# An FFT filter and a two-layer product on one core: the last output tile in one piece, one copy on another engine, and a few pieces moved

## The chip, the cores and the metric

The kernel runs on one core of one Trainium2 chip. The core has several engines that run side by side and wait for one another through semaphores. TensorE multiplies matrices; the profile calls it PE, and PEld for its weight loads. VectorE is called DVE, ScalarE ACT, GpSimd POOL and SyncE SP. In this kernel SP issues the transfers between the on-chip memory and the DRAM, and POOL issues the loads of x and of the weights and the exchanges between partitions.

The metric is device time in microseconds (us). One execution was also taken with a profiler; its "span" reaches from the first to the last instruction.

## What is computed

Two steps, the second on the output of the first (cut to what matters):

```python
def _attn_ref(x, filt_r, filt_i):            # x: (8, 3008, 256)
    X = np.fft.rfft(x, axis=1)
    Y = X * (filt_r + 1j * filt_i)[None]
    return np.fft.irfft(Y, n=x.shape[1], axis=1)

def _moe_ref(x, w_in, w_out, alpha):         # x: (24064, 256), w_in: (256, 2048)
    h = x @ w_in
    g = np.maximum(h, 0.0) + alpha * np.minimum(h, 0.0)
    return g @ w_out
```

Each of 8 batches is filtered along its sequence of 3008 by a Fourier transform, a product with a filter and the transform back. The result, seen as 24064 tokens of 256 numbers, goes through a product to 2048 numbers, a leaky rectifier with its own slope for each of these, and a product back to 256.

## The kernel before

**The filter, in four stages for each batch.** 3008 is 94 x 32, and the transform is split that way.

- Stage a ("first stage") multiplies pieces of x by a table of the 94-point transform: `piece_a` (two products, L184) for batches 1 to 3; `piece_q` (four products, L210, on sums and differences of the two halves of x, which `less` and `plus` make on VectorE) for batches 4 to 7, where the plan calls the batch `split`. Each piece fills two banks of product memory (a tile `hps`) that ScalarE copies to `asb` (L315). There are eight pieces in a batch; after each second one `save_a` or `save_q` writes a quarter of `asb` to DRAM, and `turn_a` loads it back in another order as `at` (L227).
- Stage b: `piece_b` (eight products, L238, into a tile `psF`). VectorE multiplies the result by two forms of the filter (`ww`, L245, and `uu`, L246), and POOL exchanges `ww` between partitions: it is added on the way (L250, batch 1), or copied to `sw` (L252) and added by VectorE eight steps later (L257, `piece_s`).
- Stage c: `piece_c` (eight products, L269, into an `hps` tile). ScalarE copies it to `v`; `turn_c` writes `v` to DRAM (L280), and `load_zt` loads it as `zt` (L288).
- Stage d ("last stage"): `pair_d` (eight products, L293, into `psF`) and a copy to `yT`, the input of the second step, by ScalarE or VectorE.

Batch 0 has its own, earlier form (`First`) without the way through DRAM; its last transposes (`piece_t`, L411) and `pair_d` fall into the first blocks of the second step and use `psF` too.

**The second step** goes by 48 blocks of tokens, twelve for each pair of batches, of 512 tokens each but for the sixth, of 384. A block has 16 steps; step `16 n` is the first of block `n`. In each, `up` makes one slice of h (two products, L579). Two steps share an `hps` tile, which ScalarE copies to `gtb` (L588); VectorE makes the rectifier from it (L591 twice, then L593 after each fourth step). `down` (L647) multiplies `gtb` by `w_out`, 16 products for each tile of 128 tokens, two tiles in one bank of `op`. ScalarE copies it to `osb` (L652), and `store` writes it out (L561). The work of `down` is cut into 16 units for each block, kept in a queue (`units`), and runs during the block after, a unit at a time, through `pop`.

**What sets the order.** All engines run their instructions in program order, and the program is written out by hand: `plan` lists for each step what is put between the products, in the order of the `put` calls. `plan_fft` fills it for a batch: `a_at`, `b_at`, `c_at` and `d_at` are the steps of its eight stage-a pieces, six `piece_b`, six `piece_c` and eight `pair_d`. `psum[step]` counts the pieces of a step that take an `hps` tile; from step 150 on that many units of `down` run before them and as many after them, ahead of the step's own `up`. There are two `hps` tiles, one `psF`, two `op` and three `osb`, each used in turn, so a product that writes a tile waits until the copy from it two (or one) tiles ago is over, and a copy into `osb` waits until the stores of three copies ago have landed.

For the last block `start_down(last)` orders the first three tiles of 128 tokens, and `down_halves` makes the fourth in two halves of 128 columns, each with its own product, copy (L639) and store:

```python
ends = [2, 3] if last else list(range(2, n, 2)) + [n]
...
pop(n + (step in (290, 482)))
...
blk.down_halves(3)
```

Of the kernel before, what the change touches and what calls it, by code (L numbers as in the profile page):

```python
# [11 lines left out]
FP32 = mybir.dt.float32  # L12
# [3 lines left out]
N2 = 32  # L16
NK = 24
D = 256
# [3 lines left out]
AF = mybir.ActivationFunctionType  # L22
# [33 lines left out]
def kernel(  # L56
# [10 lines left out]
    nc = tc.nc  # L67
# [11 lines left out]
    p_osb = ctx.enter_context(tc.tile_pool(name="p_osb", bufs=3))  # L79
# [23 lines left out]
    wout_s = konst.tile([128, 16, D], FP16, name="wout_s")  # L103
# [12 lines left out]
    def load_x(b, c, held=False):  # L116
        xs = p_x.tile([128, 8 * D], FP16, name="xs")
        if held:
            for r in (slice(0, 32), slice(64, 96)):
                nc.vector.memset(xs[r, 0:2], 0.0)  # L120
        if b:
            for r in (slice(0, 48), slice(48, N1)):
                nc.gpsimd.dma_start(out=xs[r], in_=xrow(b, c)[r])  # L123
        else:
            w = 8 * D // (1 + (c == 3))
            for o in range(0, 8 * D, w):
                nc.gpsimd.dma_start(out=xs[0:N1, o : o + w], in_=xrow(b, c)[:, o : o + w])
        return xs

    def load_halves(b, c):  # L130
        lo, hi = (p_x.tile([128, 8 * D], FP16, name="xs") for _ in range(2))
        nc.gpsimd.dma_start(out=lo[0:48], in_=xrow(b, c)[0:48])
        if b + 1 < NB:
            nc.gpsimd.dma_start(out=hi[0:48], in_=bass.AP(
                tensor=x.tensor, offset=x.offset + (b * NFFT + 47 * N2 + 8 * c) * D, ap=[[N2 * D, 48], [1, 8 * D]]))
        else:
            nc.gpsimd.dma_start(out=hi[0:32], in_=xrow(b, c)[47:79])
            nc.gpsimd.dma_start(out=hi[32:47], in_=xrow(b, c)[79:94])
        return lo, hi
# [12 lines left out]
    def banks(wide):  # L152
        if wide:
            return psH.tile([128, 2, 512], FP32, name="hps")
        return psF.tile([128, 2, 512], FP32, name="psF")

    def bank(kind):
        if kind == "o":
            return psO.tile([128, 2, D], FP32, name="op").rearrange("p k d -> p (k d)")
        return banks(kind == "h")[:, 0]  # L160
# [5 lines left out]
    class Fft:  # L166
# [115 lines left out]
                        in_=self.v[p : p + N2, k : k + 8])  # L282

        def load_zt(self):
            ends = (0, 8, 16, 32) if self.b == 2 else range(0, 33, 8)
            for g in range(len(ends) - 1):
                s = slice(ends[g], ends[g + 1])
                nc.sync.dma_start(out=self.zt[:, s], in_=v_dram[self.b, :, s])  # L288

        def inverse(self, pd, g, dh, mh):  # L290
# [217 lines left out]
    for kp in range(12):  # L508
        if 0 < kp < 10:
            f0.piece_b(kp + 2)  # L510
        if kp == 4:
# [5 lines left out]
            for q in range(2):  # L517
                nc.gpsimd.dma_start(
                    out=wout_s[:, 8 * q : 8 * q + 8],
                    in_=moe_w_out[1024 * q : 1024 * q + 1024].rearrange("(j p) d -> p j d", p=128))  # L520
# [27 lines left out]
    for p in range(NB // 2):  # L548
        t = 0
# [1 line left out]
            blocks.append((p, t, tn))  # L551
            t += tn

    def store(p, t0, osb, lane, lo=0, hi=D):
        t = t0
        while t < t0 + 128:
            b, r = 2 * p + t // NFFT, t % NFFT
            g, o = r // NX, r % NX
            n = min(t0 + 128 - t, NX - o)
            row = b * NFFT + (o // 4) * N2 + 4 * g  # L560
            nc.sync.dma_start(  # L561
                out=bass.AP(tensor=out.tensor, offset=out.offset + row * D + lo,
                            ap=[[N2 * D, n // 4], [D, 4], [1, hi - lo]]),
                in_=osb[t - t0 : t - t0 + n, lane, lo:hi])
            t += n

    gturn = [0]
# [1 line left out]
    class Block:  # L569
# [49 lines left out]
        def start_down(self, last, quarters=False):  # L619
            n = self.tn // 128  # L620
            if quarters:
                self.todo = [(s0, s0 + 2, si, k) for k0 in range(0, 16, 4) for s0 in range(0, n, 2)
                             for si in (s0, s0 + 1) for k in range(k0, k0 + 4)]
                return
            ends = [2, 3] if last else list(range(2, n, 2)) + [n]
            half = 12 if last else 8
            self.todo = []
            for s0, s1 in zip([0] + ends, ends):
                for ks in (range(half), range(half, 16)):
                    self.todo += [(s0, s1, si, k) for si in range(s0, s1) for k in ks]  # L630

        def down_halves(self, si):
            for lo in range(0, D, 128):
                op = bank("h")[:, 0:128]
                for k in range(16):
                    nc.tensor.matmul(op, self.gts[k][:, 128 * si : 128 * si + 128], wout_s[:, k, lo : lo + 128],
                                     start=(k == 0), stop=(k == 15))
                osb = p_osb.tile([128, 2, D], FP32, name="osb")
                nc.scalar.activation(osb[:, 0, lo : lo + 128], op, AF.Copy)  # L639
                store(self.p, self.t0 + 128 * si, osb, 0, lo, lo + 128)  # L640

        def down(self, q):
            n = self.tn // 128
# [16 lines left out]
    plan, psum = {}, {}  # L660

    def put(step, fn, *args):
        plan.setdefault(step, []).append((fn, args))

    def put_h(step, fn, *args):
        put(step, fn, *args)
        psum[step] = psum.get(step, 0) + 1

    def plan_fft(b, a_at, ta, x_at, b_at, add, c_at, d_at):
        f = Fft(b)  # L670
        split = b > 3
        for q in range(6):
            put_h(c_at[q], f.piece_c, q)
            if q % 2 == 1:
                put(c_at[q] + 1, f.turn_c, q // 2)
        put(c_at[5] + (2 if b == 1 else 1), f.load_zt)
        for q in range(6):
            put(b_at[q], f.piece_b, q, not add)
            if add:
                put(b_at[q] + add, f.piece_s, q)  # L680
        for i in range(8):
            put_h(a_at[i], f.piece_q if split else f.piece_a, i)
        for c in range(4):
            put(a_at[2 * c + 1] + split, f.save_q if split else f.save_a, c)
            if b in (2, 3):
                put(x_at[c], lambda b=b, c=c: xc.update({(b, c): load_x(b, c, b == 3 and c > 1)}))
            if split:
                x0, x1, x2 = x_at[c]
                put(x0, lambda b=b, c=c: xc.update({(b, c): load_halves(b, c)}))
                put(x1, f.less, c)  # L690
                put(x2, f.plus, c)
        w = NK // len(ta)
        for q, t in enumerate(ta):
            put(t, f.turn_a, nc.sync, w * q, w * q + w)
        for i in range(8):
            put(d_at[i], f.pair_d, i, on_act)
# [11 lines left out]
    for i in (6, 7):  # L708
        put(3, lambda i=i: on_dve(*f0.half_t(i, "o")))
    put(7, f0.pair_d, 2, on_dve)  # L710
    for g, ts, ds, te, de in ((2, (19, 24), (28, 30), (on_dve, on_dve), (on_dve, on_dve)),
                              (3, (32, 34), (36, 38), (on_act, on_act), (on_act, on_act))):
        for i in range(2):
            put(ts[i], f0.piece_t, 2 * g + i, te[i])
            put(ds[i], f0.pair_d, 2 * g + i, de[i])
# [7 lines left out]
    def d_steps(p):  # L723
# [1 line left out]

    plan_fft(1, range(16, 32, 2), [31] * 4, None, (40, 46, 52, 58, 63, 68), 0, (52, 58, 64, 70, 76, 80),
             (93, 95, 98, 101, 114, 121, 142, 154))
    plan_fft(2, (48, 54, 60, 66, 72, 74, 82, 86), [90] * 4, (39, 45, 51, 57),
             (106, 116, 126, 136, 148, 158), 7, (116, 126, 136, 148, 158, 172), d_steps(96))
    for b in range(3, NB):  # L730
        p = 96 * (b - 1)
        if b == 3:
            a_at = (106, 112, 118, 124, 130, 132, 140, 144)
            x_at = (62, 69, 113, 123)
            ta = (155, 166)
        else:
            a_at = [p - 96 + t for t in (-34, -22, 2, 2, 14, 26, 38, 50)]
# [6 lines left out]
    def pop(n):  # L744
        for _ in range(n):
            if units:
                blk, q = units.popleft()
                blk.down(q)

    last = 0  # L750
    blk = Block(0, 0, 512)
# [10 lines left out]
    step = 16  # L762

    for p, t0, tn in blocks[1:]:
        blk = Block(p, t0, tn)
        for j in range(16):
            n = psum.get(step, 0)
            if step < 150:
                pop({16: 0, 18: 2}.get(step, 1 if n else 0))
            else:  # L770
                pop(n)
            for fn, args in plan.pop(step, ()):
                fn(*args)
            if step >= 150:
                pop(n + (step in (290, 482)))
            blk.up(j)
            if n:
                last = step
            else:
                soon = any(t in psum for t in range(step + 1, step + 14))  # L780
                if not (step >= 150 and step % 2 and step - last > 2 and soon and len(units) < 18 - j):
                    pop(1)
            step += 1
        blk.start_down(step == 16 * len(blocks))
        units.extend((blk, q) for q in range(16))
    pop(len(units))
    blk.down_halves(3)
    assert not plan


# [28 lines left out]
```

## Time and profile before

| | |
|---|---|
| time, median of 3 runs | 768.16 us (766.91 to 768.26) |
| profiled execution | 767.84 us |
| its span | 766.1 us |
| PE busy | 756.4 us (99%) |
| DVE busy | 634.2 us (83%) |
| ACT busy | 582.6 us (76%) |
| POOL busy | 146.5 us (19%) |
| L647 (`down`) | 2992 products, 273 ns each |
| L579 (`up`) | 1504 products, 375 ns each |
| DMA | 100.04 MB, mean 131 GB/s |

How to read it: products overlap, so the duration of one is longer than the distance to the next one's start. "L647" is line 647 of the kernel before; `op<-wout_s,gtb` means that `op` is written from `wout_s` and `gtb`. In a timeline each line has the start, the duration, the engine, the line and the operation; like instructions in a row are drawn together (x4), and brackets hold the idle time before them and what ended it. SPq is SP's queue of transfers; its durations are those of issuing, not of the transfer.

### The profile page before, as it was taken

How to read it: one execution, taken by the hardware profiler on the slowest of the kernel's cores; microseconds unless marked ns; L12 is line 12 of the kernel's file. 1: busy time of each engine (PE TensorE's matmuls, PEld its weight loads, DVE VectorE, ACT ScalarE, POOL GpSimd, SP SyncE). 2: the span in 40 equal slices, each digit the busy share in tenths (PEclk: the TensorE clock that was granted, in tenths of full speed). 3: DMA queues.
4: the chain of work that ended last, by engine and by line, in shares of the span. 5: the costliest groups of instructions: out<-in, count | busy, mean ns of one | idle time of the engine just before them, and what ended most of it. 6: DMA issues, size and time to landing. Idle time of an engine off the chain costs nothing.

```text
span 766.1 us, 16640 instructions
## 1 busy us (share of the span) xinstructions
PE 756.4 (99%) x6569; PEld 507.7 (66%) x6569; DVE 634.2 (83%) x1163; ACT 582.6 (76%) x673; POOL 146.5 (19%) x277
## 2 busy tenths in 40 slices
PE   8999999999999999999999999999999999999997
PEld 4676667666666667666666666766666666766666
DVE  4898975889789998899888998899877888676673
ACT  4788787888788787887878787788767777776663
POOL 6620740231211220122202122112201212000000
PEclk9999999999999999999999999999999999999999
DMA  9996996565762469543864438533562213511011
GB/s 163 163 238 170 165 207 202 149 167 138 181 160 71 122 159 196 135 113 86 191 191 104 118 104 196 161 85 118 138 169 78 84 57 91 152 36 38 32 42 56
DMA packets 97518, 100.04 MB, mean 131 GB/s; under 512 B 12086, under 2 KB 83526, under 8 KB 97152
## 3 DMA queue, kind: packets, MB, share of 16 engines
q1 hardware_dynamic: 82416, 69.50, 31.2%
q0 software_dynamic: 15024, 29.49, 21.4%
q8 instruction: 51, 0.84, 0.4%
q14 instruction: 27, 0.22, 0.1%
HBM read 55.02 MB, written 46.66 MB: 133 GB/s over the span
## 4 chain that ended last, share of the span: by engine, by line
PE 89%; DVE 5%; DMA 3%; POOL 1%; ACT 1%; issue 1%; SPq 0%; DVEq 0%; ACTq 0%; POOLq 0%
PE op L647 40%; PE hps L579 39%; PE psF L293 2%; PE hps L269 2%; PE psF L238 1%; DVE m L591 1%; DVE gtb L593 1%; DMA xs<-in_x_dram 1%; PE hps L184 1%; PE hps L210 1%; DMA sw<-ww 1%; DVE gtb L616 1%; DMA filt_s<-in_filt_r_dram 1%; PE hps L602 1%; DVE m L615 1%
## 5 line engine op out<-in xcount | busy, mean ns | idle before, releaser
L588 ACT ACTIVATE gtb<-hps 128x1024 f16<-128x1024 f32 (+1 forms) x376 | 377.4, 1006 | 131.9 <-PE hps L579 129.5
L647 PE MATMUL op<-wout_s,gtb 128*128 128x256 f16 x2992 | 428.9, 273 | 0.0
L579 PE MATMUL hps<-yT,win_s 128*128 128x512 f16 (+1 forms) x1504 | 417.6, 375 | 0.0
L647 PEld LDWEIGHTS <-gtb 128*128 128x128 f16 x2992 | 289.3, 98 | 163.3 <-issue 10.7
L591 DVE TENSOR_SCALAR m<-gtb,alm_s 128x512 f16<-128x512 f16 (+1 forms) x752 | 227.1, 346 | 96.0 <-ACT gtb L588 94.5
L593 DVE TENSOR_TENSOR gtb<-gtb,m 128x2048 f16<-128x2048 f16 (+1 forms) x188 | 226.1, 1203 | 10.3
L579 PEld LDWEIGHTS <-win_s 128*128 128x128 f16 x1504 | 142.5, 98 | 54.7 <-issue 4.7
L252 POOL DMA_DIRECT2D sw<-ww x144 | 71.9, 508 | 414.3 <-DVE ww L245 399.5
L652 ACT ACTIVATE osb<-op 128x512 f32<-128x512 f32 x96 | 56.3, 586 | 11.0 <-PE op L647 9.9
L315 ACT ACTIVATE asb<-hps 128x1024 f16<-128x1024 f32 (+1 forms) x56 | 56.7, 1020 | 7.1 <-PE hps L184 5.5
L315 ACT ACTIVATE v<-hps 128x1024 f16<-128x1024 f32 (+1 forms) x43 | 43.5, 1011 | 10.9 <-PE hps L269 10.9
L245 DVE TENSOR_TENSOR ww<-psF,filts_s 128x1024 f16<-128x1024 f32 x42 | 51.2, 1218 | 0.6 <-PE hps L579 0.4
L246 DVE TENSOR_TENSOR uu<-psF,filt_s 128x1024 f16<-128x1024 f32 x42 | 51.0, 1215 | 0.0
L315 ACT ACTIVATE yT<-psF 128x752 f16<-128x752 f32 (+1 forms) x59 | 46.5, 788 | 1.6 <-PE psF L293 1.5
L293 PEld LDWEIGHTS <-zt 96*128 96x128 f16 x504 | 28.1, 98 | 6.2 <-issue 0.7
L293 PE MATMUL psF<-wi_s,zt 96*128 96x94 f16 x448 | 27.9, 205 | 0.0
L257 DVE TENSOR_TENSOR uu<-uu,sw 128x1024 f16<-128x1024 f16 x36 | 24.6, 682 | 1.6 <-DMA sw<-ww 1.6
L250 POOL DMA_DIRECT2D uu<-ww x24 | 19.2, 1160 | 28.8 <-DVE uu L246 22.8
L123 POOL DMA_DIRECT2D xs<-in_x_dram x24 | 18.4, 1003 | 12.3 <-issue 4.3
L194 DVE TENSOR_TENSOR xs<-xs 47x2048 f16<-47x2048 f16 x16 | 19.5, 1220 | 0.4
L198 DVE TENSOR_TENSOR xs<-xs 47x2048 f16<-47x2048 f16 x16 | 19.4, 1210 | 0.0
L269 PE MATMUL hps<-uu,twi_s 64*64 64x256 f16 x336 | 17.3, 281 | 0.3 <-DVE uu L257 0.2
(104 smaller groups left out, 269.5 us busy)
## 6 DMA issues: line engine op xcount, KB each, us to landing
out_dram<-osb SPq DMA_DIRECT2D x127, 128.0 KB
v_dram<-v SPq DMA_DIRECT2D x84, 128.0 KB
zt<-v_dram SPq DMA_DIRECT2D x26, 384.0 KB
sw<-ww POOLq DMA_DIRECT2D x144, 64.0 KB, 2.6
xs<-in_x_dram POOLq DMA_DIRECT2D x40, 192.0 KB, 6.7
at<-a_dram SPq DMA_DIRECT2D x40, 192.0 KB
a_dram<-asb SPq DMA_DIRECT2D x32, 192.0 KB
a_dram<-asb SPq DMA_DIRECT2D x12, 384.0 KB
```

Of the source, the lines that this page charges most:

```text
L245: nc.vector.tensor_mul(ww, px, fs)
L246: nc.vector.tensor_mul(uu, px, f)
L252: nc.gpsimd.dma_start(out=sw[o : o + 32], in_=ww[i : i + 32])
L269: nc.tensor.matmul(ps[64 * par : 64 * par + 64, e, 256 * h : 256 * h + 256], twi_s[r, 4 * q + 2 * h + par], u[r, par, h], start=True, stop ...
L293: nc.tensor.matmul(ps[:, m], self.zt[:, 8 * g + 4 * mh + m, dh * 128 : dh * 128 + 128], self.wi, start=True, stop=True)
L315: nc.scalar.activation(o, i, AF.Copy)
L579: nc.tensor.matmul(self.hps[:, j % 2, 0:tn], win_s[:, kt, j * 128 : (j + 1) * 128], yT[:, kt, self.t0 : self.t0 + tn], start=(kt == 0), st ...
L588: nc.scalar.activation(g[:, 2 * i : 2 * i + 2], self.hps[:, :, 0:tn], AF.Copy)
L591: nc.vector.tensor_scalar(m[:, 2 * i + h], g[:, 2 * i + h], 0.0, a, OP.min, OP.mult)
L593: nc.vector.tensor_add(g, g, m)
L647: nc.tensor.matmul(self.op[s0][:, si - s0], self.gts[k][:, 128 * si : 128 * si + 128], wout_s[:, k], start=(si == s0 and k == 0), stop=(si ...
L652: nc.scalar.activation(osb[:, 0:m], self.op[s0][:, 0:m], AF.Copy)
```

## The change

Six edits, each small:

1. The fourth tile of the last block is made like the third: 16 products of 256 columns into `op`, one copy, one store. `down_halves` is gone.
2. Of batch 0's four late `pair_d` copies, that of step 28 goes from VectorE to ScalarE.
3. Batch 2's last two stage-a pieces move from steps 82 and 86 to 78 and 82.
4. In batches 4 to 7, piece 2 of stage a is put at the front of its step's list, in steps 194, 290, 386 and 482. There it stands ahead of the `piece_b` of the batch before, with piece 3 still behind it.
5. The additional unit of `down` at steps 290 and 482 is gone. In TensorE's order its three products come back at the end of steps 299 and 491.
6. Batch 2's `zt` is loaded in four quarters like that of the others, not in two quarters and a half.

On TensorE 32 products of 128 columns become 16 of 256; all others stay, some at other places. VectorE has one copy fewer and ScalarE the same number.

```diff
-            ends = (0, 8, 16, 32) if self.b == 2 else range(0, 33, 8)
-            for g in range(len(ends) - 1):
-                s = slice(ends[g], ends[g + 1])
+            for g in range(4):
+                s = slice(8 * g, 8 * g + 8)
                 nc.sync.dma_start(out=self.zt[:, s], in_=v_dram[self.b, :, s])
...
-            ends = [2, 3] if last else list(range(2, n, 2)) + [n]
+            ends = [2, 3, 4] if last else list(range(2, n, 2)) + [n]
...
-        def down_halves(self, si):
-            for lo in range(0, D, 128):
-                op = bank("h")[:, 0:128]
-                for k in range(16):
-                    nc.tensor.matmul(op, self.gts[k][:, 128 * si : 128 * si + 128], wout_s[:, k, lo : lo + 128],
-                                     start=(k == 0), stop=(k == 15))
-                osb = p_osb.tile([128, 2, D], FP32, name="osb")
-                nc.scalar.activation(osb[:, 0, lo : lo + 128], op, AF.Copy)
-                store(self.p, self.t0 + 128 * si, osb, 0, lo, lo + 128)
...
             put_h(a_at[i], f.piece_q if split else f.piece_a, i)
+            if split and i == 2:
+                plan[a_at[2]].insert(0, plan[a_at[2]].pop())
...
-    for g, ts, ds, te, de in ((2, (19, 24), (28, 30), (on_dve, on_dve), (on_dve, on_dve)),
+    for g, ts, ds, te, de in ((2, (19, 24), (28, 30), (on_dve, on_dve), (on_act, on_dve)),
...
-    plan_fft(2, (48, 54, 60, 66, 72, 74, 82, 86), [90] * 4, (39, 45, 51, 57),
+    plan_fft(2, (48, 54, 60, 66, 72, 74, 78, 82), [90] * 4, (39, 45, 51, 57),
...
-                pop(n + (step in (290, 482)))
+                pop(n)
...
     pop(len(units))
-    blk.down_halves(3)
```

`store` loses the arguments `lo` and `hi` that only the halves used.

More of the change, by code (lines that the diff above doesn't have):

```diff
@@ L552, with store @@
             t += tn
-    def store(p, t0, osb, lane, lo=0, hi=D):
+    def store(p, t0, osb, lane):
         t = t0
@@ L561, in store @@
             nc.sync.dma_start(
-                out=bass.AP(tensor=out.tensor, offset=out.offset + row * D + lo,
-                            ap=[[N2 * D, n // 4], [D, 4], [1, hi - lo]]),
-                in_=osb[t - t0 : t - t0 + n, lane, lo:hi])
+                out=bass.AP(tensor=out.tensor, offset=out.offset + row * D,
+                            ap=[[N2 * D, n // 4], [D, 4], [1, D]]),
+                in_=osb[t - t0 : t - t0 + n, lane])
             t += n
```

## The prediction

> **What bounds the kernel now.** I read the page first (busy times, chain by engine), then the chain's end, then the timeline at each place that the change touches.
>
> ```profile
> PE 756.4 (99%) x6569; PEld 507.7 (66%) x6569; DVE 634.2 (83%) x1163; ACT 582.6 (76%) x673; POOL 146.5 (19%) x277
> ...
> PE 89%; DVE 5%; DMA 3%; POOL 1%; ACT 1%; issue 1%; SPq 0%; DVEq 0%; ACTq 0%; POOLq 0%
> ```
>
> TensorE is busy for 756.4 of 766.1 us and has 89% of the chain. So an edit counts where it opens or closes a gap between products, or behind the last product. Unhindered, an L647 starts every (6.28 - 0.27)/55 = 0.109 us (the 56 from 753.69 on) and an L579 every (1.03 - 0.38)/3 = 0.217; gaps below are counted against that.
>
> The chain's end, then the timeline there (start, duration, engine, what; in brackets the idle time before and what ended it):
>
> ```profile
> 760.29 2.57 DMA out_dram<-osb
> ...
> 762.96 0.28 ACT osb L639
> ```
>
> ```profile
> 759.80 1.95 PE L636 MATMUL hps<-wout_s,gtb 128*128 128x128 f16 x32
> 760.05 0.38 ACT L652 ACTIVATE osb<-op 128x256 f32<-128x256 f32 x1 [1.15 <-PE op L647]
> ...
> 762.96 0.28 ACT L639 ACTIVATE osb<-hps 128x128 f32<-128x128 f32 x1 [1.74 <-DMA out_dram<-osb]
> ```
>
> The last copy waits 1.74 us, not for its products (over at 761.75) but for a store that still reads the output tile which it reuses.
>
> Steps 28 to 30, the one long gap of the first blocks:
>
> ```profile
> 58.70 0.93 DVE L318 CAST yT<-psF 128x752 f16<-128x752 f32 x1
> ...
> 59.69 0.49 PE L293 MATMUL psF<-wif_s,zt 96*128 96x94 f16 x8 [0.49 <-DVE yT L318]
> ...
> 60.65 1.02 ACT L315 ACTIVATE asb<-hps 96x1024 f16<-96x1024 f32 x1 [0.74 <-PE hps L184]
> ```
>
> Around step 93 (batch 1's loads of zt, then its first last-stage product):
>
> ```profile
> 119.84 1.83 SPq L288 DMA_DIRECT2D zt<-v_dram  x4
> ...
> 124.03 0.50 PE L293 MATMUL psF<-wi_s,zt 96*128 96x94 f16 x8
> ```
>
> No wait shows, but the last of the sixteen semaphore updates of the first of these loads is at 123.76: only 0.27 us to spare.
>
> **The change, part by part.**
>
> *Last tile in one piece: -0.88.* Two halves (32 products of 128 columns) become 16 of 256, at the same rate: the last starts at 759.80 + 15 x 0.109 = 761.43 and ends 0.27 later, at 761.71. With one copy fewer, the ring of three output tiles gives the last copy the tile of the copy at 754.81, whose stores have landed by 759.16; the wait goes. The copy starts 0.08 behind the product (760.05 against 759.97) and takes 0.38 like its neighbour: over at 762.17 instead of 763.24, 1.07 sooner. SP is free at 761.86. The store has 128 KB instead of 64: 2.08 us from issue to landing (stores at 749.54 and 761.29) instead of 1.89 (763.27), 0.19 longer. Ends: -1.07 (store as quick as the small one) and -0.39 (as slow as the one at 760.29, 2.57).
>
> *Copy of step 28 by ScalarE: -0.50.* The product's last L293 ends at 57.02 and ScalarE is then free, so the copy starts at 57.06, not at 58.70 behind VectorE's add (L593). It holds ScalarE 0.68 us (spacing of the yT at 318.70 to the next L588), of which 0.43 lay idle there (57.06 to the asb at 57.49): the asb starts at 57.74, the L588 at 58.66 instead of 58.41, over at 59.67. TensorE reaches step 30's L293 at 59.03 and, with psF free, saves 0.66; its L579 at 59.79 finds the bank of that L588 free. Late next is VectorE: the L591 pair now waits for that L588 (59.71), the second copy starts at 60.36 instead of 60.22 and ends at 61.31, and step 32's L411, which needs psF, starts at 61.36 instead of 61.10 (now: 61.76): 0.40 left. The next gap there (0.10 at 64.03, waiting for a zt copy by ScalarE) closes, since ScalarE runs 0.5 ahead: 0.50. Ends: 0 and -0.66. The transfers behind it move along: the save of step 30 goes out 0.15 sooner, and the at loads needed at 70.45 had landed at 69.05.
>
> *Batch 2's pieces at 78 and 82 instead of 82 and 86: +0.26.* Step 86 loses two L184 (2 x 0.217 = 0.43), step 78 gains them. ScalarE then copies at each even step from 70 to 82. Gaps now: 0.105 before 115.40, 0.086 before 116.56, 0.185 before 120.23, each TensorE waiting for ScalarE to free a bank. By the same spacings (0.91 an L588, 0.48 the osb, 0.90 the v) there would be 0.16 at step 82, 0.04 at 84, none at 88: 0.17 gained, were the products all. But step 80's L269 now stands behind the piece, at 113.41 instead of 112.98; its copy to v follows the step-78 L588 (112.70, behind the new asb at 111.78) and an osb copy, at 114.09 instead of 113.61; and SP's v_dram writes, three stores and the zt loads form one unbroken queue from 114.67 to 121.67, so the first zt load lands at 123.76 + 0.48 = 124.24. L293 could start at 124.03 - 0.17 = 123.86 and waits until 124.29. Ends: -0.17 (the load lands in time) and +0.43 (nothing of step 86's saving comes through). On SP the save of the last piece still stands behind the zt loads, at loads of batch 2 (landed 132.44, needed 135.74) are covered, and the x quarter that step 78 needs was issued at 89.46.
>
> *One piece in front of piece_b, at 194, 290, 386, 482; one unit fewer at 290 and 482: -0.41.* At 194 and 290:
>
> ```profile
> 222.58 1.94 ACT L315 ACTIVATE asb<-hps 128x1024 f16<-128x1024 f32 x2 [0.37 <-PE hps L210]
> ...
> 223.65 1.02 PE L579 MATMUL hps<-yT,win_s 128*128 128x512 f16 x4
> ```
>
> ```profile
> 313.02 1.16 PE L647 MATMUL op<-wout_s,gtb 128*128 128x256 f16 x9
> ...
> 314.01 1.03 PE L579 MATMUL hps<-yT,win_s 128*128 128x512 f16 x4
> ```
>
> At 194 the L579 waits 0.10 for the first asb copy (over at 223.60). That piece now runs 0.25 us ahead (221.89 instead of 222.14), so the copy ends at 223.35 and the gap closes; 386 has the same gap (405.20): -0.21. VectorE's L245 moves back 0.22; its exchange copies land 2.4 us before they are read. At 290 nine L647 just cover the copy. Now six do, to 313.67, and the copy, 0.24 sooner, frees the bank at 313.76: a new gap of 0.09. TensorE, ScalarE and VectorE then run 0.25 ahead until the three products come back at step 299. That is spent at step 302: its L269 waits 0.12 for VectorE's add (L257, over at 322.98), its L210 0.18 for a bank (an L588 over at 323.61); both end sooner, and the L579 at 324.68 is kept back only by the copy of v. I take -0.10 each at 290 and 482 (ends: +0.08, the new gap alone, and -0.21, all of the relief).
> One handover is new: L210 then L238. Nearest rows: L238 then L210 costs nothing (starts of successive products: 24 places, 0 but for two bank waits), L647 then L238 0.095. I take nothing, because both use quarter tiles of 64 columns as in the first row; the other end is 4 x 0.095 = +0.38. The Trainium skill, "TensorEngine Tiling (Array Packing)", Key Properties, says that changing the tiling mode, not the tile, drains the engine. The 0.095 at L647/L238 and 0 at L238/L210 agree; were 47 rows against 64 a change of mode, the sum would be -1.15 instead of -1.53.
>
> *Batch 2's zt in four loads: 0.* One more issue (0.42 us) on SP before three stores; ScalarE's copies have three tiles in turn, and the pieces split apart landed at 217.63, first read 30 steps after the issue. Ends: 0 and +0.4, the issue uncovered.
>
> **Sum:** -0.88 - 0.50 + 0.26 - 0.21 - 0.20 = -1.53. The profiled execution took 767.84 us (span 766.1), so 766.3; it lies 0.32 under the median of 768.16, so on that basis **766.6**. A difference of 0.2%, 1.54 us, is about what a measurement of this kernel tells from none: 766.62 is that border.
>
> **Rivals.**
> A. The sum as it stands: 766.6, own range 766.0 to 767.2.
> B. The zt wait stays out and step 302 gives all its relief: +0.26 becomes -0.17, -0.20 becomes -0.42: 766.0. For: the seven first zt loads took 3.61 to 3.92 us, and this one's 3.92 is the longest. Against: the 0.27 to spare.
> C. The early gains don't last: batch 1's exchange transfers are just in time (last landing 82.68, its L269 at 82.70; the next late one 112.78 against 112.98) and hold the products there. The 0.50 goes: 767.1. For: those two rows. Against: they are issued by VectorE's work, which moves along.
> D. The change doesn't do what it says at the end: the last copy would wait for something other than the ring. Then the larger copy and store cost 0.10 + 0.19 instead of gaining 0.88: 767.8. Against: the chain names the store and the waiting instruction ends 0.02 behind its landing.
> E. Slower: batch 1's first zt load lands as late as the save issued 1.88 us behind it in that queue (121.72 to 128.98, 7.26 us, against 3.92). L293 waits 3.3 us more: 769.9. It decides from 1.5 us of delay, slower by over 0.2% from 3.1. For: nothing is spare there any more, and the queues are full. Against: the order on SP is unchanged and the other six took 3.8 at most.
>
> **How the numbers follow.** A 0.42, B 0.24, C 0.15, D 0.05, E 0.14. Half of A and nearly all of B lie under 766.62: faster 0.45; the rest of A, C and D: same 0.41; E: slower 0.14. The range leaves out E and the lower end of B: 765.5 (the low ends together, -0.66 for step 28 among them: -2.53, so 765.6) to 768.3 (no gain at all, 768.2).
>
> **What would show it.** Right: the last osb copy with no wait for a DMA, over some 1.1 us before its present place; no gap at step 30's L293 but some 0.2 at step 32's L411; L293 of step 93 waiting some 0.4 for a DMA; no gap at the L579 of 194 and 386, 0.09 at 290 and 482 with smaller ones at 302 and 494; TensorE's rate as now. Wrong: a wait at step 93 of over 1 us, 0.095 at L210/L238, or waits at L269 of steps 52 or 80.

## The result, and the profile after

The changed kernel takes 765.70 us (median of 16 runs, 765.32 to 768.17); the kernel before, run beside it, 767.94 us (16 runs, 766.91 to 769.17). The ratio is 0.9973 with a 95% interval of 0.9966 to 0.9981: 2.24 us or 0.27% faster, 1.46 to 2.61 by the interval. The forecast was 1.53 less, within 765.5 to 768.3. The two profiled executions differ by 1.80 (766.04 against 767.84), their spans by 1.84.

The page of the changed kernel, busy times and chain by engine:

```profile
PE 756.1 (99%) x6553; PEld 507.6 (66%) x6553; DVE 633.0 (83%) x1162; ACT 583.2 (76%) x673; POOL 146.1 (19%) x277
...
PE 96%; DMA 2%; POOL 2%; ACT 0%; issue 0%; POOLq 0%; ACTq 0%
```

TensorE is as busy as before (756.1 against 756.4), so what went is time between and behind its products. Its share of the chain is 96% instead of 89%: VectorE, which held steps 28 to 30, is no longer in the chain. The second number must not be read as time won; the chain of before took VectorE's own work for long stretches that cost no wait.

I compare the start of the same L579 product (L578 after the change: lines behind the edits have moved up) in the two traces. "Shift" is after minus before in us; minus is sooner:

| stretch | shift behind it | gained or lost there | forecast |
|---|---|---|---|
| start, to step 28 | +0.22 | +0.22 | - |
| steps 30 to 34 (edit 2) | -0.38 | -0.60 | -0.50 |
| steps 78 to 93 (edit 3) | -0.32 | +0.06 | +0.26 |
| step 194 (edit 4) | -0.42 | -0.10 | -0.10 |
| steps 290 to 304 (edits 4, 5) | -0.51 | -0.09 | -0.10 |
| step 326 | -0.77 | -0.26 | - |
| step 386 (edit 4) | -0.86 | -0.09 | -0.10 |
| steps 482 to 496 (edits 4, 5) | -0.96 | -0.10 | -0.10 |
| behind the last product (edit 1) | -1.84 | -0.88 | -0.88 |

The edits make -1.80 of it. The two rows without a forecast nearly cancel, and neither is an effect of the change that I can show: the first arises in the startup, in code that no edit touches, and the second was one late exchange copy in the execution before (below). All of these are readings of single executions, but the stretches of the edits repeat: edit 2 gives 0.59 to 0.60 in each of the seven profiled kernels that have it, edit 4 0.09 to 0.10 at 194 and at 386 in each of eight. From the start of step 767's product to the last landing it is 11.01 to 11.02 in the seven kernels with edit 1 and 11.87 to 11.90 in the six with the old tail.

**The tail.** The end of the chain and the timeline there, after the change:

```profile
752.89 7.87 PE op L636 x72
...
760.84 0.39 ACT osb L641
```

```profile
755.78 4.97 PE L636 MATMUL op<-wout_s,gtb 128*128 128x256 f16 x44
...
759.09 0.39 ACT L641 ACTIVATE osb<-op 128x256 f32<-128x256 f32 x1 [1.15 <-PE op L636]
760.84 0.39 ACT L641 ACTIVATE osb<-op 128x256 f32<-128x256 f32 x1 [1.36 <-PE op L636]
```

No transfer stands in the chain's end any more. The last copy starts 0.09 behind the last product (755.78 + 4.97 = 760.75), released by it and not by a store. Its store is issued at 761.25 and lands at 763.31, 2.06 later.

**Steps 28 to 34.** ScalarE, then TensorE:

```profile
57.28 0.80 ACT L314 ACTIVATE yT<-psF 128x752 f16<-128x752 f32 x1 [0.22 <-PE psF L292]
57.97 1.01 ACT L314 ACTIVATE asb<-hps 96x1024 f16<-96x1024 f32 x1
58.88 1.02 ACT L587 ACTIVATE gtb<-hps 128x1024 f16<-128x1024 f32 x1
```

```profile
58.38 1.04 PE L636 MATMUL op<-wout_s,gtb 128*128 128x256 f16 x8
59.25 0.50 PE L292 MATMUL psF<-wif_s,zt 96*128 96x94 f16 x8
...
61.45 0.61 PE L410 MATMUL psF<-ids,v 128*96 128x128 f16 x8
```

The yT copy stands where VectorE's add no longer delays it, the 0.49 gap ahead of step 30's L292 is gone (59.25 = 58.38 + 8 x 0.109), and step 32's L410 is only slightly late.

**Steps 82 to 93.** SyncE's queue before and after (start, duration), then step 93's weight loads, whose first reads zt:

```profile
114.67 2.52 SPq L280 DMA_DIRECT2D v_dram<-v  x4
```

```profile
114.75 1.88 SPq L280 DMA_DIRECT2D v_dram<-v  x4
...
119.30 1.82 SPq L287 DMA_DIRECT2D zt<-v_dram  x4
```

```profile
123.70 0.36 PEld L292 LDWEIGHTS <-zt 96*128 96x128 f16 x8 [0.36 <-DMA zt<-v_dram]
```

The wait for zt that the forecast put at 0.43 is there, between products 0.25. The four v_dram writes were issued in 1.88 us instead of 2.52 (the second one took 0.44, before 1.13), so the zt load went out at 119.30; it landed at 123.66, 4.36 after its issue, against 3.92 before.

**Steps 194 and 290.** TensorE:

```profile
222.35 1.05 PE L636 MATMUL op<-wout_s,gtb 128*128 128x256 f16 x8
223.24 1.03 PE L578 MATMUL hps<-yT,win_s 128*128 128x512 f16 x4
...
311.82 0.41 PE L210 MATMUL hps<-xs,wfq_s 47*64 47x512 f16 x4
312.06 0.39 PE L238 MATMUL psF<-at,twf_s 64*64 64x256 f16 x8
312.28 0.39 PE L210 MATMUL hps<-xs,wfq_s 47*64 47x512 f16 x4
312.60 0.83 PE L636 MATMUL op<-wout_s,gtb 128*128 128x256 f16 x6
313.36 1.02 PE L578 MATMUL hps<-yT,win_s 128*128 128x512 f16 x4
```

At 194 the L578 follows the eight L636 without a gap (222.35 + 8 x 0.109 = 223.22; before, there were 0.10 between them). At 290 six L636 now stand ahead of the L578, and the gap behind them is 0.09, as forecast. The new handover from L210 to L238 costs next to nothing: the four L210 take 0.24 to the start of what follows when that is an L238 (311.82 to 312.06), 0.22 when it is four more L210 (in the kernel before), and 0.32 when it is an L636 (312.28 to 312.60), a handover that costs 0.10.

### The profile page after: what moved, and what is told of

The parts are those of the page before. It is cut to its first block, busy times and chain, and to the rows that moved or that the text cites. A ratio compares the mean times of both kernels' runs of the same rounds, so it can differ in the third digit from the quotient of the medians.

```text
span 764.2 us, 16602 instructions
## 1 busy us (share of the span) xinstructions
PE 756.1 (99%) x6553; PEld 507.6 (66%) x6553; DVE 633.0 (83%) x1162; ACT 583.2 (76%) x673; POOL 146.1 (19%) x277
## 4 chain that ended last, share of the span: by engine, by line
PE 96%; DMA 2%; POOL 2%; ACT 0%; issue 0%; POOLq 0%; ACTq 0%
PE op L636 43%; PE hps L578 42%; PE psF L292 3%; PE hps L269 2%; PE hps L184 1%; PE psF L238 1%; DMA xs<-in_x_dram 1%; POOL filt_s L147 1%; PE hps L210 1%; PE hps L601 1%; DMA zt<-v_dram 1%; PE psF L410 0%; PE op L394 0%; POOL xs L127 0%; ACT v L314 0%
## 5 line engine op out<-in xcount | busy, mean ns | idle before, releaser
L636 PE MATMUL op<-wout_s,gtb 128*128 128x256 f16 x3008 | 430.9, 273 | 0.0
L578 PE MATMUL hps<-yT,win_s 128*128 128x512 f16 (+1 forms) x1504 | 417.7, 375 | 0.0
L636 PEld LDWEIGHTS <-gtb 128*128 128x128 f16 x3008 | 291.1, 98 | 163.1 <-issue 10.3
L578 PEld LDWEIGHTS <-win_s 128*128 128x128 f16 x1504 | 142.6, 98 | 54.8 <-issue 4.4
L641 ACT ACTIVATE osb<-op 128x512 f32<-128x512 f32 (+1 forms) x97 | 56.6, 583 | 12.3 <-PE op L636 11.2
L292 PEld LDWEIGHTS <-zt 96*128 96x128 f16 x504 | 28.0, 98 | 5.5 <-DMA zt<-v_dram 0.4
L292 PE MATMUL psF<-wi_s,zt 96*128 96x94 f16 x448 | 27.9, 205 | 0.1
```

What stands on the lines that cost most here:

```text
L292: nc.tensor.matmul(ps[:, m], self.zt[:, 8 * g + 4 * mh + m, dh * 128 : dh * 128 + 128], self.wi, start=True, stop=True)
L578: nc.tensor.matmul(self.hps[:, j % 2, 0:tn], win_s[:, kt, j * 128 : (j + 1) * 128], yT[:, kt, self.t0 : self.t0 + tn], start=(kt == 0), st ...
L636: nc.tensor.matmul(self.op[s0][:, si - s0], self.gts[k][:, 128 * si : 128 * si + 128], wout_s[:, k], start=(si == s0 and k == 0), stop=(si ...
L641: nc.scalar.activation(osb[:, 0:m], self.op[s0][:, 0:m], AF.Copy)
```

## The experiments

Each of these was timed in five rounds against the kernel before, which took 768.13 to 768.37 us in the four comparisons. An interval is some 0.18% wide, 1.4 us. That is more than any single edit is forecast to give, so the verdicts rest on shifts in the profiled execution, counted as in the table above, and the times say whether the whole agrees.

### Each edit alone

**Edit 1, the last tile in one piece.**

```diff
-            ends = [2, 3] if last else list(range(2, n, 2)) + [n]
+            ends = [2, 3, 4] if last else list(range(2, n, 2)) + [n]
...
     pop(len(units))
-    blk.down_halves(3)
```

> The kernel before with edit 1 alone (last tile in one piece). Ring theory: up to the last block nothing moves; the last copy follows its products by 0.08 us with no wait for a store, ends some 1.07 us sooner, and the span behind the last product shrinks so that the whole is 0.88 us shorter. Rival (the last copy waits for something other than the ring of output tiles): the wait of some 1.2 us stays and the larger copy and store add 0.3.

768.15 us, ratio 0.9998 (0.9989 to 1.0007). In its timeline:

```profile
761.26 0.38 ACT L652 ACTIVATE osb<-op 128x256 f32<-128x256 f32 x1 [1.15 <-PE op L647]
763.00 0.38 ACT L652 ACTIVATE osb<-op 128x256 f32<-128x256 f32 x1 [1.36 <-PE op L647]
```

The wait for the store is gone. The execution reached the end of its products 1.21 us later than the kernel before, for reasons earlier in it, yet its last store landed only 0.32 later (765.48 against 765.16): the tail gave 0.89. The time neither confirms nor excludes it: -0.88 would be a ratio of 0.9989, at the very edge of the interval. What ate the gain in the profiled execution was the start (+0.35), a wait of 0.19 for zt at step 93 and above all a wait at step 52:

```profile
83.06 0.30 PE L269 MATMUL hps<-uu,twi_s 64*64 64x256 f16 x2
84.01 0.41 PE L269 MATMUL hps<-uu,twi_s 64*64 64x256 f16 x6 [0.65 <-DMA uu<-ww]
```

The first stage-c product of batch 1 lost 0.93 us between its second and third instruction until an exchange copy had landed. The tail is the last thing that the edit could have moved; nothing of it lies there. This wait is followed up below.

**Only the ring, with the halves kept.** Both halves write one output tile, so that the ring of three is enough, and nothing else changes:

```diff
         def down_halves(self, si):
+            osb = p_osb.tile([128, 2, D], FP32, name="osb")
             for lo in range(0, D, 128):
...
-                osb = p_osb.tile([128, 2, D], FP32, name="osb")
```

> The kernel before, the last tile still in two halves, but both halves copied into one output tile, so that the second half doesn't need the tile of the copy three before. Ring theory: the second copy starts 0.09 us behind the last product (761.75), ends at 762.12 instead of 763.24; SP is issuing the first half's store until 762.53, so the last store starts 0.7 us sooner than now and the whole is 0.7 us shorter, a little less than in one piece (0.88). Rival (two halves are slow by themselves, or the wait is another): no change.

767.84 us, ratio 0.9993 (0.9984 to 1.0002). The timeline:

```profile
762.16 0.28 ACT L639 ACTIVATE osb<-hps 128x128 f32<-128x128 f32 x1 [0.51 <-PE hps L637]
763.00 0.28 ACT L639 ACTIVATE osb<-hps 128x128 f32<-128x128 f32 x1 [0.57 <-PE hps L637]
```

Here too the second copy follows its product. The products ended 1.22 later than before and the last store landed 0.57 later: 0.65 gained. So the wait was for the ring; the one piece gives 0.24 more, because with two halves three stores stand one behind the other on SyncE's queue (issued at 762.51, 763.17 and 763.83) and the last waits for its turn.

**Edit 2, the copy of step 28 by ScalarE.**

```diff
-    for g, ts, ds, te, de in ((2, (19, 24), (28, 30), (on_dve, on_dve), (on_dve, on_dve)),
+    for g, ts, ds, te, de in ((2, (19, 24), (28, 30), (on_dve, on_dve), (on_act, on_dve)),
```

> The kernel before with edit 2 alone (step 28's copy by ScalarE). Theory: the gap before step 30's first last-stage product goes, 0.2 to 0.3 us of it come back as a wait at step 32's transpose, and from step 34 on every product is 0.5 to 0.6 us sooner than in the kernel before, to the end. Rival C (exchange transfers hold the products): the lead is gone by step 80, with waits at the stage-c products of steps 52 to 80.

767.48 us, ratio 0.9988 (0.9979 to 0.9996), the only single edit whose interval leaves out 1. Shift +0.45 at step 28, -0.20 at 30, -0.08 at 32, -0.14 at 34: -0.59. The lead did not last in this execution: at step 52 the shift goes from -0.15 to +0.35, because the first stage-c product waits for an exchange copy. That is the sign that was named for rival C:

```profile
83.07 0.41 PE L269 MATMUL hps<-uu,twi_s 64*64 64x256 f16 x6 [0.22 <-DMA uu<-ww]
```

The same wait stands in kernels without this edit (tail in one piece, halves in one tile), whose code is that of the kernel before up to the last block, and it is missing in the changed kernel; more on it below. The end is as in the kernel before, with the same wait:

```profile
763.03 0.28 ACT L639 ACTIVATE osb<-hps 128x128 f32<-128x128 f32 x1 [1.72 <-DMA out_dram<-osb]
```

**Edit 3, batch 2's pieces at 78 and 82**, alone, and the reverse: the changed kernel with the pieces at 82 and 86 again.

```diff
-    plan_fft(2, (48, 54, 60, 66, 72, 74, 82, 86), [90] * 4, (39, 45, 51, 57),
+    plan_fft(2, (48, 54, 60, 66, 72, 74, 78, 82), [90] * 4, (39, 45, 51, 57),
```

> The kernel before with edit 3 alone (batch 2's last two pieces at steps 78 and 82). Theory: the three gaps of 0.1 to 0.2 us at steps 82, 84 and 88 shrink to some 0.15 in all, but step 93's first last-stage product waits for batch 1's first zt load; behind it the products are later than in the kernel before by 0 to 0.4 us, 0.26 if SP's second v_dram issue takes 1.1 us as in the kernel before, less if it takes 0.44 as in the changed kernel. Rival (only ScalarE's copies count): no wait for the load, 0.17 sooner.

> The changed kernel with batch 2's pieces back at 82 and 86. Theory: no wait for the zt load at step 93, the gaps at 82, 84 and 88 as in the kernel before; it was worth 0.06 us in the profiles, so within 0.3 us of the changed kernel, rather sooner. Rival (only ScalarE's copies count): 0.17 us later than the changed kernel.

Alone: 768.53 us, ratio 1.0001 (0.9992 to 1.0010). A load of `at` landed late at step 40 (+0.82). At step 93 zt was there in time, by 0.08 us, and the edit's whole saving came through: shift 1.15 ahead of it, 0.97 behind it, -0.18. The reverse: 766.09 us, ratio 0.9978 (0.9969 to 0.9987). Its shift is -0.37 at step 34 and still -0.37 at step 93; the changed kernel goes from -0.38 to -0.32. So in the changed kernel the edit costs 0.06, and the two times cannot be told apart. The saving is real (0.18 in both), and a wait for zt can take it back. Whether it does is not a matter of TensorE being early, since the zt loads go out behind its products: with the edit the first zt load is issued 10.26 to 10.34 us behind the start of step 76's product, in this late execution (10.26) as in the others, and 9.81 with the pieces at 82 and 86 again. What differed is the time from issue to landing: 4.10 us in the execution without a wait, 4.24 to 4.44 in the three with one.

**Edits 4 and 5, apart and together.** A piece in front of `piece_b` at 194, 290, 386 and 482; and the unit fewer at 290 and 482.

```diff
             put_h(a_at[i], f.piece_q if split else f.piece_a, i)
+            if split and i == 2:
+                plan[a_at[2]].insert(0, plan[a_at[2]].pop())
```

```diff
-                pop(n + (step in (290, 482)))
+                pop(n)
```

> The kernel before with edit 4 alone (piece 2 in front of piece_b; the additional units at 290 and 482 stay). Theory: the 0.10 gap before the up product of steps 194 and 386 goes, 0.10 each; at 290 and 482 there is no gap to close, and the waits of 0.12 and 0.18 at steps 302 and 494 stay: 0.2 us sooner in all. The handover from piece to piece_b costs nothing. Rival (it is a change of mode like the one from down to piece_b): 0.095 at each of four places, and with it 0.2 us later in all.

> The kernel before with edit 5 alone (no additional unit at 290 and 482; the pieces in the old order). Theory: six down products end 0.34 us before the bank is free, so the up product of step 290 waits 0.34; the three products come back at step 299, and of these 0.34 the waits of step 302 take back 0.1 to 0.3, so that each place makes it 0.05 to 0.25 us later. Rival (the unit is worth nothing): no difference behind step 302.

> The kernel before with piece 2 in front and the unit fewer, together. Theory: the two belong together: with the piece in front, the six products that are left cover the copy but for 0.09 us, and the relief at steps 300 to 304 comes through. Shift of the product starts against the kernel before: -0.10 at 194, -0.10 over 290 to 304, -0.10 at 386, -0.10 over 482 to 496, -0.4 in all, time 767.6 to 768.0 beside 768.15. Rival: they add up as they measured alone (front: -0.10, 0, -0.10, 0; one unit fewer: +0.13 at 290 to 304 and +0.13 at 482 to 496): -0.10, +0.13, -0.10, +0.13, together +0.06, time 768.1 to 768.3.

| | 194 | 290 to 304 | 386 | 482 to 496 | sum | time, ratio |
|---|---|---|---|---|---|---|
| piece in front only | -0.10 | 0 | -0.09 | 0 | -0.19 | 767.99, 1.0004 (0.9994 to 1.0013) |
| unit fewer only | 0 | +0.13 | 0 | +0.13 | +0.25 | 768.35, 1.0006 (0.9998 to 1.0015) |
| both | -0.10 | -0.09 | -0.09 | -0.09 | -0.37 | 767.80, 0.9995 (0.9986 to 1.0003) |

They do not add: apart they make +0.06, together -0.37. The three timelines of TensorE at step 290 show why. Piece in front only, unit fewer only, both:

```profile
315.28 1.16 PE L647 MATMUL op<-wout_s,gtb 128*128 128x256 f16 x9
316.27 1.03 PE L579 MATMUL hps<-yT,win_s 128*128 128x512 f16 x4
```

```profile
312.21 0.60 PE L210 MATMUL hps<-xs,wfq_s 47*64 47x512 f16 x8
312.74 0.83 PE L647 MATMUL op<-wout_s,gtb 128*128 128x256 f16 x6
313.72 1.02 PE L579 MATMUL hps<-yT,win_s 128*128 128x512 f16 x4
```

```profile
313.99 0.83 PE L647 MATMUL op<-wout_s,gtb 128*128 128x256 f16 x6
314.75 1.02 PE L579 MATMUL hps<-yT,win_s 128*128 128x512 f16 x4
```

With the piece in front and nine L647, the products cover the copy with nothing left over (315.28 + 9 x 0.109 = 316.26): the copy's head start buys nothing. With six L647 and the piece not in front, the L579 waits 0.31 behind them, nearly as much as the three products take (0.327). With both the wait is 0.09. (From the start of the last L647 to that of the L579 it is 0.42 and 0.20, and 0.11 without a wait.) In either kernel with six, TensorE gets the three products back at step 300 (+0.33) and 0.24 of relief at step 302; only the one that paid little at 290 comes out ahead.

### The waits for transfers

**Batch 1's loads of zt one step sooner**, in the changed kernel:

```diff
-        put(c_at[5] + (2 if b == 1 else 1), f.load_zt)
+        put(c_at[5] + 1, f.load_zt)
```

> The changed kernel with batch 1's zt loads one step sooner, so that SP issues them right behind the v_dram writes and ahead of three stores. Theory: the first load is issued some 0.8 us sooner, the wait of 0.25 us at step 93 goes, and all behind it is 0.25 us sooner than in the changed kernel; the stores behind have tiles to spare. Rival (the wait is the load's own length under the other transfers, whatever the queue): no change; or the stores that now stand behind the loads hold a copy into the ring, and it is later.

766.11 us, ratio 0.9973 (0.9962 to 0.9983). The wait at step 93 is gone: the shift is +0.39 at step 88 and stays. But this execution stood 0.96 at step 52 and came to step 93 late, so the missing wait alone does not show that the sooner loads removed it. What the trace does show is room: the first load, issued 1.92 us behind the v_dram writes instead of 2.67, landed 1.02 us ahead of its product, and 0.82 ahead in the other kernel with the sooner loads (below), against 0.08 with the pieces alone, an execution that ran still later. The time is no better than the changed kernel's.

**Batch 2's second load of x away from the exchange.** The waits at step 52 are for the fourth of the exchange copies that GpSimd issues at some 77 us; it issues that load of x (192 and 184 KB) right behind them. I moved the load ahead of the exchange in the changed kernel, by itself, then with the sooner zt loads, then held back to 70 us:

```diff
-    plan_fft(2, (48, 54, 60, 66, 72, 74, 78, 82), [90] * 4, (39, 45, 51, 57),
+    plan_fft(2, (48, 54, 60, 66, 72, 74, 78, 82), [90] * 4, (39, 39, 51, 57),
```

> The changed kernel, with batch 2's second load of x put at step 39 instead of 45, so that GpSimd issues it behind the first x load (at some 56.7 us) and no longer right behind the first exchange of batch 1. Theory: the fourth exchange copy, which step 52's first stage-c product reads, lands late because the x load (368 KB, issued 0.5 us behind it) shares the queues with it; without it the copies land within 11.2 us of the start of step 40's product (11.07 to 13.19 in the runs so far, 12.25 being the last moment), no wait shows at step 52, and the time is 765.3 to 765.7. Rival: the stores and SyncE's loads of the same stretch do it; the landing stays anywhere from 11 to 13.2, and the time is 765.7 to 766.1. Second rival: the load now lies beside the last save and the loads of at of batch 1 (issued 61.8 and 65.3, landed 0.8 us before step 40 reads them) and holds step 40 by 0.5 us or more; the time is then 766.2 or more.

> The same, and batch 1's loads of zt one step sooner, so that the 0.25 us wait at step 93 goes too. If both waits go and nothing takes their place, this is the fastest: 765.1 to 765.6. If the sooner loads of zt only make SyncE's stores late (the changed kernel with them alone took 766.1 against 765.7 for the changed kernel), 765.5 to 766.1.

The held one has this too, which puts two small VectorE writes into the tile ahead of the load:

```diff
-                put(x_at[c], lambda b=b, c=c: xc.update({(b, c): load_x(b, c, b == 3 and c > 1)}))
+                put(x_at[c], lambda b=b, c=c: xc.update({(b, c): load_x(b, c, (b, c) in ((2, 1), (3, 2), (3, 3)))}))
```

> The changed kernel, with batch 2's second load of x put at step 39 and held by two small VectorE writes there (the way in which batch 3's third and fourth loads are held already), so that it is issued at some 69.5 us: behind the loads of at that step 40 reads and about 6 us ahead of the exchange that step 52 reads. Theory: the waits at steps 40 and 52 are both a matter of which transfers lie ahead in the queues. Then the last asb save is issued at 61.8 and landed by 65.5 as in the changed kernel (66.98 with the load at 56.7), the fourth of the loads of at lands before step 40 reads it, the exchange copies land within 12.2 us of step 40's product, neither step waits, and the time is 765.2 to 765.8. Rival: the startup's spread decides these landings and not the x load; then one of the two waits shows again (0.4 to 0.95 us), and the time is 765.7 to 766.3, as of the changed kernel and its other variants. Against the theory, too: the load now lies beside the at loads of steps 46 and later; if these come late, step 46's product (75.7 us) waits.

| | fourth exchange copy landed, after step 40's product began | wait at step 40 | wait at step 52 | time, ratio |
|---|---|---|---|---|
| load at step 39 | 11.69 | 0.5 | 0 | 766.32, 0.9976 (0.9967 to 0.9986) |
| the same, zt sooner | 10.87 | 0 | 0 | 766.19, 0.9977 (0.9967 to 0.9987) |
| load held to 70.56 us | 10.70 | 0 | 0 | 766.39, 0.9975 (0.9964 to 0.9987) |

In the first, the second rival's sign came true. The load lay beside the last save of `asb`, which landed at 66.98 instead of 65.20; the loads of `at` went out at 67.10 instead of 65.32, and step 40 waited:

```profile
70.14 0.30 PE L238 MATMUL psF<-at,twf_s 64*64 64x256 f16 x2
70.67 0.41 PE L238 MATMUL psF<-at,twf_s 64*64 64x256 f16 x6 [0.24 <-DMA at<-a_dram]
```

In the second they went out as late (67.16), but this execution reached step 40 0.68 later, because of its startup, and did not wait. That the load of x made the save late is not shown either: with the pieces at 78 alone and the load at its old place, the same save landed at 67.95. The first one also lost 0.2 within the stage-c product of step 80, which started at 113.62, ahead of the landing of batch 1's last exchange copy (113.80).

In the held one neither wait shows (there is one of 0.12 for zt at step 93), and its span is the shortest profiled, 764.0 against 764.2, yet its time is not below the changed kernel's. All three expected 765.1 to 765.8 and none got there. So the theory that these waits set the time, and that the load of x makes them, is not borne out. Among the kernels with the load at its old place the landing lies between 10.89 and 13.19 and has to be under 12.25; five of these eleven profiled executions waited at step 52 (tail in one piece, halves in one tile, copy by ScalarE, piece in front, zt sooner) and one at step 40 (pieces at 78). Three without a wait at step 52 are too few to say that the load is the cause. No version beat the changed kernel.

## Why the prediction was right, and where it was off

**The mechanism held; the size was somewhat short.** A, the sum as it stands, is what the profile shows: -1.80 by the stretches of the edits, against -1.53. The measured -2.24 has an interval that holds both (1.46 to 2.61). The time itself, 765.70, lies below A's own range (766.0 to 767.2) and only 0.2 above the lower end of the whole range. Of the 0.9 that it lies under the forecast 766.6, 0.22 is the base (the forecast stood on 768.16, and the kernel before took 767.94 beside it), 0.27 is in the sum, above all in two terms that were mis-sized, the copy at step 28 and the pieces at 78 and 82, and some 0.44 is not explained: the median moved that much more than the profiled executions. Single executions of one kernel differ by 2 to 3 us. So the total is in part luck; the parts, below, are what the prediction can be judged by.

**The tail (-0.88): right to 0.01**, and right in its parts. The copy starts 0.09 behind the product instead of 1.2 (the prediction took 0.08), and its 128 KB store takes 2.06 from issue to landing (taken: 2.08). D is out: the wait was for the ring, as the halves in one tile show by themselves.

**The copy at step 28 (-0.50): -0.60 in the changed kernel, -0.59 alone.** The term was mis-sized at step 32. Step 30 gave 0.65 (0.66 forecast), but L410 of step 32 kept a loss of 0.12 against step 30 where I had 0.26. I had put VectorE's second copy 0.65 behind the start of the L591 pair; the pair starts when I said (59.93, that is 59.71 + 0.22) and the copy 0.53 behind it, at 60.46. The closing of the small gap two steps later gave 0.07, where 0.10 was forecast.

**The pieces at 78 and 82 (+0.26): +0.06**, mis-sized. The products' saving was 0.18 (forecast 0.17). The wait for zt was 0.25, not 0.43. The step that failed is "form one unbroken queue from 114.67 to 121.67, so the first zt load lands at 123.76 + 0.48 = 124.24". The 0.48 was right: it is the difference between 9.81 and 10.29 us behind step 76's product. But I moved the queue's issues as a block with the durations of the one profile, and the longest of them, 1.13 us for the second v_dram write, was 0.44 this time. The landing in turn took 0.44 longer than the 3.92 that I kept; in the fourteen profiled executions this load took 3.89 to 4.56, so that 3.92 was near the short end. Both durations vary from execution to execution, so a slack of 0.27 us was no figure to work with to the second digit. The bounds (-0.17 and +0.43) hold to 0.01: alone, where zt was in time, the edit gave -0.18. B is half true: the wait shrank but did not stay out.

**194 and 386 (-0.21 together): -0.19. 290 and 482 (-0.10 each): -0.09 and -0.10**, with the 0.09 gap where it was expected. The gaps named at steps 302 and 494 are there too, 0.09 each and not smaller: at 302 the L578 starts at 324.12, 0.20 behind the start of the last of six L636, where 0.11 is a product's own. The waits for VectorE's add and for the bank are gone (0.12 and 0.18, and 0.02 behind them), so that a relief of 0.24 is left at 302, of which 0.05 was given back at step 304. The prediction treated the two edits as one term, and that was needed: alone one gives nothing there and the other costs 0.13.

**The handover L210 to L238: 0.02 where 0 was taken**, at all four places: from the start of the last L210 it is 0.23 to the L238, against 0.21 to another group of L210 and 0.31 to an L636. The Trainium skill, "TensorEngine Tiling (Array Packing)", Key Properties, lets a change of mode drain the engine and not a change of tile. The trace agrees if 47 rows beside 64 are no change of mode: 0.02 beside 0.10.

**zt in four loads: 0.** No shift shows between steps 93 and 194 but for edit 4's.

**C** (batch 1's exchange holds the products) did not happen in the changed kernel's profile, but the row it was read from was the right one: landings "just in time" did turn into waits of 0.5 to 0.96 at step 52, and with the copy by ScalarE alone such a wait took the lead away. What C had wrong is the cause. They came in three of the seven kernels without edit 2 that have the load of x at its old place, and in two of the four with it, so it is no answer to TensorE being early. What makes the fourth exchange copy late is open.

**E** (a late zt load costs 3.3) did not happen. The longest wait at step 93 in any profiled execution was 0.69 us, in the kernel with edits 4 and 5 only, whose TensorE stood 0.4 later than before and not earlier. There the second v_dram write took 1.84 to issue, and all behind it on SyncE's queue moved:

```profile
125.09 0.51 PE L293 MATMUL psF<-wi_s,zt 96*128 96x94 f16 x8 [0.52 <-DMA zt<-v_dram]
```

**Not in the sum at all:** -0.26 at step 326, which the prediction passed over because the wait is in the kernel before and no edit touches it. In the execution before, the exchange copies issued from 337.88 had landed only at 345.68, VectorE's add waited for them, and TensorE for it:

```profile
345.81 0.69 DVE L257 TENSOR_TENSOR uu<-uu,sw 128x1024 f16<-128x1024 f16 x1 [0.46 <-DMA sw<-ww]
```

```profile
346.55 0.41 PE L269 MATMUL hps<-uu,twi_s 64*64 64x256 f16 x8 [0.18 <-DVE uu L257]
```

The last of these copies took 6.20 us to land there, and 3.83 to 4.90 in the thirteen other kernels. All of them, edited or not near there, miss this wait and gain some 0.25: a stall that one profile shows once may be that execution's own.

## What to carry to other kernels

Where the last copy of a kernel waits for a store, look at the ring of buffers first: freeing one tile paid its computed price, 0.88 us within 0.01 in one piece and 0.65 of 0.7 in two. Two edits that each do nothing or harm may be one edit (a copy started sooner, and the cover above it cut to match): price them together and try them together. A slack of a few tenths ahead of a transfer is a chance and not a number: issue and landing times of the same transfer moved by more than that between executions, and where single edits are worth less than the spread of the time, the shift of the same instruction between two traces tells what the medians cannot.

## What the runs showed of the hardware that I had not expected

- SyncE's second v_dram write of the burst at 115 us took 0.44 us to issue in the changed kernel, 1.13 in the kernel before and 1.84 with edits 4 and 5 only; with the tail in one piece the third took 1.11. What it waited for was not tried.
- The fourth exchange copy (64 KB, GpSimd, added on the way) took 3.95 us from issue to landing in the kernel with the held load (76.73 to 80.68), 4.32 in the changed kernel, 5.47 before and 6.43 with the sooner zt loads, at the same place in the program.
- The startup, whose code no edit touches, moved the first blocks by -0.23 to +1.84 us against the kernel before.
